# A gated state-space and product-key mixture on one core: one-hot products as 64-row products on the two row halves

## Chip, core and metric

The kernel runs on one core of one Trainium2 chip. The metric is device time in microseconds (us) of one execution. Before the change it is 1450.14 us, the median of 3 runs (1449.04 to 1450.3).

## The reference, cut to what matters

Two branches of the same 2048 tokens of 576 channels are mixed by a gate. Branch A is a diagonal state-space convolution of length 2048, branch B picks for each token and each of 32 heads 2 of 4096 experts by product keys:

```
s1, s2 = q1 @ k1.T, q2 @ k2.T             # 64 scores each, top 2 of each
top_e, g = best 2 of the 4 sums, softmax   # e = 64 * i1 + i2
act = gelu(x @ u[top_e])
out_B = sum over 32 heads and 2 picks of g * act * v[top_e]
out = sigmoid(x . gate_w) * out_A + (1 - gate) * out_B
```

The kernel doesn't gather experts. It computes x @ u.T for all 4096 experts, applies gelu, multiplies by a matrix of weights G[token, expert] that is zero but for the picked experts, and multiplies the result by all of v.

## The kernel before, in words

The program is written in Python that keeps its own clock: helpers add to it what each product should cost (`mm`, L207), tasks are generators that wait on that clock (`ready`, `need`), and so the order of each engine's instructions is fixed when the program is built. A changed cost or a changed duration in this model moves instructions.

Matmuls on TensorE carry short names in the profile: `a` is x @ u.T, `s` the scores of the product keys, `kP`, `kb`, `k`, `u`, `pr`, `pi`, `pv`, `y` belong to branch A's convolution, `tr` turns the picked indices and weights, `S` makes the matrix G, and `o` is the last product, with v. Until about 995 us `s`, `a` and branch A's stages share TensorE. After that it runs `o`, token block by token block (16 blocks t of 128 tokens, 32 groups b of 128 experts, three products for high and low parts, two halves of 288 columns), and between the `o` of one block it makes the `S` of a later one.

For a block t, `prep(t)` (L1498) loads gl, the 128 x 4096 values of x @ u.T, applies gelu, and goes through four quarters q of 32 tokens. For each quarter `onehot(t, q)` (L1485) lets VectorE write three tables. Partitions hold the picks: those of 16 tokens of the block's first half on partitions 0 to 63 (32 heads x 2 picks), those of 16 tokens of its second half on partitions 64 to 127. A is the one-hot of 128 row indices, Be the one-hot of the column index, and Bg is Be times the high and times the low part of the pick's weight. Be and Bg are 64 columns wide: `iota_b` is shifted by 32 in the lower partitions, so that a pick of partitions 0 to 63 can only hit columns 0 to 31 and one of partitions 64 to 127 only columns 32 to 63. One product with all 128 rows and 64 columns therefore makes G for two tokens. A quarter has 16 such pairs of tokens with two products each (high and low, accumulated), 32 in a block, in two PSUM banks (`pS`). VectorE then multiplies gl by them straight from PSUM, four instructions of 256 elements a quarter, and frees the banks. Two banks of tag `wb` are needed for a quarter, four are there. Tables of quarter q + 2 are written after quarter q's multiplications. At the end gl is split in f16 high and low parts, wh, the weights of `o`.

Of the kernel before, what the change touches and what calls it, by code (L numbers as in the profile page):

```python
# [13 lines left out]
F16 = mybir.dt.float16  # L14
# [4 lines left out]
OP = mybir.AluOpType  # L19
# [119 lines left out]
def body(ctx: ExitStack, tc: tile.TileContext, xT, au, par, logdt, dskip, gatew, wq, kT, uT, vv,  # L139
# [17 lines left out]
    def key(x):  # L157
        n = x.tensor.name
        return (n, x.offset) if n in columns else n

    def size(x):
        n = 1
        for d in x.shape[1:]:
            n *= d
        return n
# [30 lines left out]
    S = Engine(nc.scalar, rdy, clock, key, act_cost)  # L196
    V = Engine(nc.vector, rdy, clock, key, dve_cost)
    G = Engine(nc.gpsimd, rdy, clock, key, lambda op, o, a, k: 0.15 + 0.0021 * size(o))

    def dma(o, i, q=None):  # L200
        t = max(clock[0], rdy.get(key(i), 0.0), queue[0])
        queue[0] = t + 0.45
        wire[0] = max(wire[0], t) + (2 if o.dtype in (F16, BF16) else 4) * o.shape[0] * size(o) / 3.4e5
        rdy[key(o)] = max(rdy.get(key(o), 0.0), wire[0] + 2.2)
        (q or DQ).dma_start(o, i)

    def mm(o, l, r, start, stop, cost=None):  # L207
        m = l.shape[0] > 64, 128 if size(l) > 64 else size(l)
        if m != tiling[0]:
            tiling[0] = m  # L210
            clock[0] += 0.13 if m == (True, 128) else 0.1
        clock[0] += (size(r) * (4 if r.dtype == F32 else 1) / 2400 + 0.003) if cost is None else cost
        rdy[key(o)] = clock[0] + 0.4
        T.matmul(o, l, r, start=start, stop=stop)  # L214

    def spawn(gen, after=0.0):
        heapq.heappush(heap, (clock[0] + after, nseq[0], gen))
        nseq[0] += 1
# [49 lines left out]
    def take(tag, name):  # L268
        lst = slots[tag]
        assert lst, name  # L270
        lst.remove(min(lst))
# [18 lines left out]
    def bank(tag, name):  # L290
        take(tag, name)
        t = ps.tile([128, 512], F32, tag="ps", name=name, bufs=8)
        banks.add(t.tensor.name)
        return t
# [30 lines left out]
    cst = cp.tile([128, KT], F32, name="cst")  # L325
# [652 lines left out]
    ab = iota_a = iota_b = None  # L978
# [286 lines left out]
    def freq():  # L1265
        nonlocal ff, ab, iota_a, iota_b
        ff = FG.__enter__()
        wrems.append(ff.tile([128, 2, 512], F16, name="wrem3"))
        V.memset(wrems[3][64:128, 1, :], 0.0)
        ksb = KS.__enter__().tile([128, 4, NCK // 2, 32, 2 * NI], F16, name="ksb")  # L1270
        fk = FK.__enter__()
        tabs = [fk.tile([128, 16, 2, 128], F16, tag="tk", name=f"tk{w0}", bufs=2) for w0 in (0, 16)]
        for w0, tkt in zip((0, 16), tabs):
            dma(tkt, tk_d[:, w0:w0 + 16, :])
        for j in range(4):
            while wire[0] > clock[0] + 2:
                yield 0.3
            dma(ksb[:, j].rearrange("p c w i -> p c (w i)"),
                k_d[:, 32 * j:32 * j + 32].rearrange("c l z m n -> (l z m) c n"))
        spawn(v_norm(), 12)  # L1280
        spawn(gating(0), 20)
        yield from k_stage1(ksb, fk, tabs)
        FK.__exit__(None, None, None)
        KS.__exit__(None, None, None)
        v_pool(0, 3)
        spawn(v_work())
        fp = FP.__enter__()
        quota(sc=3, wb=5)
        yield 3
        spawn(prep(0))  # L1290
        yield from products(fp)
        FP.__exit__(None, None, None)
        quota(sc=4, wb=4)
        ab = ctx.enter_context(tc.tile_pool(name="ab", bufs=1, side="right"))
        iota_a = ab.tile([128, 128, 2], F16, name="iota_a")
        iota_b = ab.tile([128, 64, 2], F16, name="iota_b")
        V.tensor_copy(iota_a, cst[:, 384:512, None].to_broadcast([128, 128, 2]))
        V.tensor_copy(iota_b, cst[:, 512:576, None].to_broadcast([128, 64, 2]))
        iotas.append(1)
        v_pool(3, 5)  # L1300
        while not gated or not gates:
            yield 0.5
        FG.__exit__(None, None, None)
        WJ.__exit__(None, None, None)
        v_pool(5, 8)
        shut.append(1)
# [178 lines left out]
    def onehot(t, q):  # L1485
        def ib(r, m):
            v = idxT[:, t, r, 16 * q:16 * q + 16].rearrange("p (a k) -> p a k", k=2)
            return v[:, :, None, :].to_broadcast([128, 8, m, 2])
        A = ab.tile([128, 8, 128, 2], F16, tag="A1", name=f"A1{t}_{q}", bufs=2)
        V.tensor_tensor(out=A, in0=iota_a[:, None].to_broadcast([128, 8, 128, 2]), in1=ib(0, 128), op=OP.is_equal)  # L1490
        Be = ab.tile([128, 8, 64, 2], F16, tag="Be", name=f"Be{t}_{q}", bufs=1)
        V.tensor_tensor(out=Be, in0=iota_b[:, None].to_broadcast([128, 8, 64, 2]), in1=ib(1, 64), op=OP.is_equal)
        Bg = ab.tile([128, 2, 8, 64, 2], F16, tag="Bg", name=f"Bg{t}_{q}", bufs=2)
        for z in range(2):
            V.tensor_tensor(out=Bg[:, z], in0=Be, in1=ib(2 + z, 64), op=OP.mult)
        return A, Bg

    def prep(t):  # L1498
        while stored[t // 4] < 32 or groups:
            yield 1  # L1500
        yield from need("slot", 2)
        gl = [slot([16, 128], F32, f"gl{t}_{h}") for h in range(2)]
        for h in range(2):
            dma(gl[h], g_d[t][:, 16 * h:16 * h + 16])
        if t != ORDER[0]:
            while t not in placed:
                yield 0.3
            oh = {0: onehot(t, 0), 1: onehot(t, 1)}
        yield from ready(*gl)
        for h in range(2):  # L1510
            for b0 in (0, 8):
                g = gl[h][:, b0:b0 + 8]
                S.activation(g, g, AF.Gelu_apprx_tanh)
        if t == ORDER[0]:
            while t not in placed or not iotas:
                yield 0.3
            oh = {0: onehot(t, 0), 1: onehot(t, 1)}
        for q in range(4):
            A, Bg = oh.pop(q)
            yield from ready(A, Bg)  # L1520
            yield from need("wb", 2)
            pbs = []
            for hb in range(2):
                pS = bank("wb", f"S{t}_{q}_{hb}")
                for j in range(8):
                    a, k = 4 * hb + j // 2, j % 2
                    for z in range(2):
                        mm(pS[:, 64 * j:64 * j + 64], A[:, a, :, k], Bg[:, z, a, :, k], z == 0, z == 1)
                pbs.append(pS)
                del pS  # L1530
            yield from ready(*pbs)
            for hb, pS in enumerate(pbs):
                n0 = 16 * q + 8 * hb
                pv = pS.rearrange("p (k r b) -> p b r k", r=2, b=32)
                for h in range(2):
                    gv = gl[h].rearrange("p b (r n) -> p b r n", r=2)[:, :, :, n0:n0 + 8]
                    V.tensor_tensor(out=gv, in0=pv[:, 16 * h:16 * h + 16], in1=gv, op=OP.mult)
                free("wb", *gl)
            del pbs, pS, pv
            if q < 2:  # L1540
                oh[q + 2] = onehot(t, q + 2)
        if t != ORDER[-1]:
            spawn(prep(ORDER[ORDER.index(t) + 1]))
        h = []
        for z in range(2):
            yield from need("slot")
            h.append(slot([32, 128], F16, f"wh{t}_{z}"))
        fl = lambda x: x.rearrange("p b n -> p (b n)")
        for q in range(4):
            bs = slice(8 * q, 8 * q + 8)  # L1550
            src = gl[q // 2][:, 8 * (q % 2):8 * (q % 2) + 8]
            if t in ORDER[:2] and V.free > clock[0] + 6 and max(G.free, S.free) < clock[0] + 1:
                S.activation(fl(h[0][:, bs]), fl(src), AF.Copy, scale=s_wg)
                S.activation(fl(src), fl(src), AF.Copy, scale=s_wg)
                yield from ready(h[0], *gl)
                G.tensor_sub(fl(h[1][:, bs]), fl(src), fl(h[0][:, bs]))
            else:
                yield from split(fl(h[0][:, bs]), fl(h[1][:, bs]), fl(src), s_wg)
            yield 0.3
        free("slot", h[1])  # L1560
        free("slot", h[1])
        st[t] = h
# [147 lines left out]
    for w, n in ((0, 9), (1, 5)):  # L1710
        for xk in [x for k in range(4) for x in (k, 4 + k)[:2 - w]] + [8]:
            k = 4 if xk == 8 else xk % 4
# [12 lines left out]
    while groups or acts:  # L1725
# [5 lines left out]
        if groups and bank_free() and lag < (6.0 if not a_ok else 2.0 if not turn_s else 5.0 if kdone[0] < NCK else 8.0):  # L1731
            c, t = groups[0]
# [9 lines left out]
        if acts and bank_free():  # L1742
            c, tb, j = acts[0]
# [31 lines left out]
    for t in ORDER:  # L1775
        until(lambda: t in st)
        h = st.pop(t)
# [70 lines left out]
```

## Time and profile before

| | |
|---|---|
| median of 3 runs | 1450.14 us |
| lowest, highest | 1449.04, 1450.3 us |
| span of the profiled execution, first to last instruction | 1447.6 us |
| TensorE products / loads | 14105 / 14105 |
| S products | 2048 in 64 blocks, between 955 and 1391 us |
| o products | 3072 |

The profiled execution is one of its own; its time beside the span is not recorded, and its span is 2.5 us below the median of the runs. In the rows of the profile PE is TensorE's products, PEld its weight loads, DVE is VectorE, ACT ScalarE, POOL GpSimd. A group's row gives the tile written and those read, the shape, the count, then busy us, the mean ns of one, and the idle time of the engine just ahead of it with what ended it. In a product's shape `128*128` stands for the rows and columns of the weights. Ends of matmuls are modelled.

### The profile page before, as it was taken

The numbers are of one execution on the slowest core, as the hardware profiler recorded it, in microseconds if no ns is written. First come the engines' busy times: TensorE is split into PE (matmuls) and PEld (weight loads), VectorE is DVE, ScalarE is ACT, GpSimd is POOL, SyncE is SP. The second block draws the span as 40 slices with busy tenths as digits, with TensorE's granted clock in tenths as the row PEclk, the third lists the DMA queues.
The fourth block names the chain that finished last, engine by engine and source line by source line (L and its number), as shares of the span: only waits on it lengthen the run. The fifth ranks groups of instructions, "written<-read, shape, count | busy, mean of one in ns | idle before, by whom it ended". The sixth has DMA issues, their size and how long they took to land.

```text
span 1447.6 us, 36680 instructions
## 1 busy us (share of the span) xinstructions
PE 1426.9 (99%) x14105; PEld 852.3 (59%) x14105; DVE 1208.5 (83%) x4598; ACT 769.6 (53%) x1285; POOL 481.5 (33%) x491
## 2 busy tenths in 40 slices
PE   7999999999999999999999999999999999999998
PEld 3444445455455445445555444456887887888787
DVE  6899899889877997885899897589999988888850
ACT  6346876796684776844656655655434223323310
POOL 0325357547356436220547899600000000000000
PEclk9999999999999999999999999999999999999999
DMA  8235323342324333169675777776543333342400
GB/s 308 74 117 159 96 74 120 125 143 72 117 93 150 95 105 99 49 199 293 209 272 179 255 256 270 267 259 210 196 127 111 108 120 107 123 145 68 157 10 17
DMA packets 134351, 215.42 MB, mean 149 GB/s; under 512 B 10912, under 2 KB 79904, under 8 KB 127776
## 3 DMA queue, kind: packets, MB, share of 16 engines
q1 hardware_dynamic: 134080, 213.01, 45.5%
q8 instruction: 110, 1.80, 0.5%
q14 instruction: 65, 0.53, 0.1%
q10 hardware_dynamic: 96, 0.07, 0.0%
HBM read 141.74 MB, written 71.30 MB: 147 GB/s over the span
## 4 chain that ended last, share of the span: by engine, by line
PE 89%; DMA 2%; DVE 2%; issue 0%; ACT 0%; SPq 0%; ACTq 0%; DVEq 0%
PE o L214 26%; PE s L214 24%; PE a L214 23%; PE S L214 4%; PE kb L214 2%; PE pr L214 2%; PE wb L214 2%; PE y L214 1%; PE kP L214 1%; PE pv L214 1%; PE u L214 1%; PE k L214 1%; DMA z_d<-vo 1%; DMA ksb<-k_d 1%; DVE i L134 1%; DMA vn<-in_au_dram 0%
## 5 line engine op out<-in xcount | busy, mean ns | idle before, releaser
L214 PE MATMUL o<-vhl,wh 128*128 128x288 f16 x3072 | 387.0, 286 | 0.0
L214 PE MATMUL s<-whl,xb 128*128 128x512 f16 x1536 | 363.9, 379 | 0.0
L214 PE MATMUL a<-xb,uhl 128*128 128x512 f16 x1536 | 359.7, 379 | 0.2 <-DVE go L134 0.2
L214 PEld LDWEIGHTS <-wh 128*128 128x128 f16 x3072 | 296.0, 98 | 76.3 <-issue 3.7
L214 PEld LDWEIGHTS <-xb 128*128 128x128 f16 x1792 | 170.6, 98 | 210.1 <-issue 15.3
L214 PEld LDWEIGHTS <-uhl 128*128 128x128 f16 x1536 | 147.3, 98 | 176.2 <-issue 3.4
L134 DVE FIND_INDEX8 i<-m,s 128x8 uint32<-128x64 f32 x1024 | 206.5, 222 | 0.0
L134 ACT ACTIVATE wh<-gl,s_wg 128x1024 f16<-128x1024 f32 x64 | 68.9, 1137 | 202.3 <-DVE gl L134 202.3
L134 DVE MAX8 m<-s 128x8 f32<-128x64 f32 x1024 | 146.3, 215 | 29.3 <-PE s L214 28.4
L134 POOL TENSOR_TENSOR CS<-CS,ex 128x512 f32<-128x512 f32 x72 | 98.0, 1393 | 147.6 <-DVE ex L134 146.2
L134 ACT ACTIVATE go<-a,i_a 128x512 f32<-128x512 f32 x94 | 63.2, 685 | 96.4 <-PE a L214 68.6
L134 DVE TENSOR_TENSOR gl<-S,gl 128x256 f32<-128x256 f32 x256 | 90.5, 416 | 12.6 <-PE S L214 8.3
L134 POOL TENSOR_TENSOR e<-aN,rt 128x512 f32<-128x512 f32 x72 | 83.2, 1177 | 49.9 <-PE kb L214 43.7
L134 DVE SCALAR_TENSOR_TENSOR wh<-gl,s_wg,wh 128x1024 f16<-128x1024 f32 x63 | 78.6, 1280 | 10.7 <-ACT wh L134 10.7
L134 DVE TENSOR_TENSOR Bg<-Be,vals 128x1024 f16<-128x1024 f16 x128 | 84.6, 702 | 2.2
L134 ACT ACTIVATE gl<-gl 128x1024 f32<-128x1024 f32 x64 | 63.5, 1045 | 34.2 <-DMA gl<-g_d 31.1
L134 DVE TENSOR_TENSOR A<-iota_a,vals 128x2048 f16<-128x2048 f16 x64 | 77.9, 1216 | 0.0
L214 PE MATMUL s<-wrem,xb 128*128 128x512 f16 x256 | 76.2, 379 | 0.0
L214 PE MATMUL a<-xb,wrem 128*128 128x512 f16 x256 | 75.9, 379 | 0.0
L214 PEld LDWEIGHTS <-A 128*128 128x128 f16 x2048 | 70.5, 97 | 4.7
L134 DVE MATCH_VALUE_LOAD i<-m,s 128x8 f32 x1024 | 72.6, 71 | 0.1
L214 PE MATMUL S<-Bg,A 128*128 128x64 f16 x2048 | 72.3, 193 | 0.0
(205 smaller groups left out, 2068.5 us busy)
## 6 DMA issues: line engine op xcount, KB each, us to landing
g_d<-go SPq DMA_DIRECT2D x128, 256.0 KB, 2.5
gl<-g_d SPq DMA_DIRECT2D x32, 1024.0 KB, 5.4
wq<-in_wq_dram SPq DMA_DIRECT2D x16, 1152.0 KB, 6.0
su_d<-us SPq DMA_DIRECT2D x32, 288.0 KB, 2.6
sk_d<-k1o SPq DMA_DIRECT2D x32, 288.0 KB, 2.9
ui<-su_d SPq DMA_DIRECT2D x16, 576.0 KB, 4.0
ki<-sk_d SPq DMA_DIRECT2D x16, 576.0 KB, 5.3
vn<-in_vv_dram SPq DMA_DIRECT2D x32, 288.0 KB, 5.4
```

Of the source, the lines that this page charges most:

```text
L134: return f(*a, **k)
L214: T.matmul(o, l, r, start=start, stop=stop)
```

## The change

The two halves of the partitions are multiplied apart. A product uses 64 rows, of partitions 0 to 63 or 64 to 127, and 32 columns, and makes G for one token; there are 64 products a quarter instead of 32, those of the upper rows writing one bank and those of the lower rows the other, by turns. The second tables Be and Bg are 32 columns wide, since a half no longer needs the zero columns of the other, and `iota_b` is the same in all partitions. The order within a block is: token pair, high or low part, row half. The helper is given 0.014 us as the cost of one product. The multiplications of gl go over one bank for each row half, 16 x 16 elements, still four of 256.

```diff
-        iota_b = ab.tile([128, 64, 2], F16, name="iota_b")
+        iota_b = ab.tile([128, 32, 2], F16, name="iota_b")
...
-        V.tensor_copy(iota_b, cst[:, 512:576, None].to_broadcast([128, 64, 2]))
+        V.tensor_copy(iota_b, cst[:, 384:416, None].to_broadcast([128, 32, 2]))
...
-        Be = ab.tile([128, 8, 64, 2], F16, tag="Be", name=f"Be{t}_{q}", bufs=1)
-        V.tensor_tensor(out=Be, in0=iota_b[:, None].to_broadcast([128, 8, 64, 2]), in1=ib(1, 64), op=OP.is_equal)
-        Bg = ab.tile([128, 2, 8, 64, 2], F16, tag="Bg", name=f"Bg{t}_{q}", bufs=2)
+        Be = ab.tile([128, 8, 32, 2], F16, tag="Be", name=f"Be{t}_{q}", bufs=1)
+        V.tensor_tensor(out=Be, in0=iota_b[:, None].to_broadcast([128, 8, 32, 2]), in1=ib(1, 32), op=OP.is_equal)
+        Bg = ab.tile([128, 2, 8, 32, 2], F16, tag="Bg", name=f"Bg{t}_{q}", bufs=2)
         for z in range(2):
-            V.tensor_tensor(out=Bg[:, z], in0=Be, in1=ib(2 + z, 64), op=OP.mult)
+            V.tensor_tensor(out=Bg[:, z], in0=Be, in1=ib(2 + z, 32), op=OP.mult)
...
-            for hb in range(2):
-                pS = bank("wb", f"S{t}_{q}_{hb}")
-                for j in range(8):
-                    a, k = 4 * hb + j // 2, j % 2
-                    for z in range(2):
-                        mm(pS[:, 64 * j:64 * j + 64], A[:, a, :, k], Bg[:, z, a, :, k], z == 0, z == 1)
-                pbs.append(pS)
-                del pS
+            pbs = [bank("wb", f"S{t}_{q}_{r}") for r in range(2)]
+            for j in range(16):
+                for z in range(2):
+                    for r, pS in enumerate(pbs):
+                        rows = slice(64 * r, 64 * r + 64)
+                        mm(pS[:, 32 * j:32 * j + 32], A[rows, j // 2, :, j % 2], Bg[rows, z, j // 2, :, j % 2],
+                           z == 0, z == 1, 0.014)
             yield from ready(*pbs)
-            for hb, pS in enumerate(pbs):
-                n0 = 16 * q + 8 * hb
-                pv = pS.rearrange("p (k r b) -> p b r k", r=2, b=32)
+            n0 = 16 * q
+            for r, pS in enumerate(pbs):
+                pv = pS.rearrange("p (k b) -> p b k", b=32)
                 for h in range(2):
-                    gv = gl[h].rearrange("p b (r n) -> p b r n", r=2)[:, :, :, n0:n0 + 8]
+                    gv = gl[h].rearrange("p b (r n) -> p b r n", r=2)[:, :, r, n0:n0 + 16]
                     V.tensor_tensor(out=gv, in0=pv[:, 16 * h:16 * h + 16], in1=gv, op=OP.mult)
                 free("wb", *gl)
```

## Prediction

> **What bounds the kernel now.** I read the page first: busy shares and the chain that ended last.
>
> ```profile
> PE 1426.9 (99%) x14105; PEld 852.3 (59%) x14105; DVE 1208.5 (83%) x4598; ACT 769.6 (53%) x1285; POOL 481.5 (33%) x491
> PE 89%; DMA 2%; DVE 2%; issue 0%; ACT 0%; SPq 0%; ACTq 0%; DVEq 0%
> L214 PE MATMUL o<-vhl,wh 128*128 128x288 f16 x3072 | 387.0, 286 | 0.0
> L214 PE MATMUL S<-Bg,A 128*128 128x64 f16 x2048 | 72.3, 193 | 0.0
> core 0: 1447.6 us, clock 1.000
> ```
>
> The last number of the two group rows is the idle time of TensorE ahead of them: 0.0. The one-hot products S and the products o around them never wait for VectorE, though VectorE is nearly as full. The table by stage, for the stretch in which tokens are done one after another:
>
> ```profile
> 1015.00:1100.00 85.00, 85.00 (x1062) 68.82 (x1061) 82.51 (x140) 30.99 (x33) 0.00 (x0) 1.00 0.41 131
> 1200.00:1300.00 100.00, 100.00 (x1197) 81.22 (x1188) 88.68 (x146) 29.61 (x30) 0.00 (x0) 1.00 0.39 128
> ```
>
> The columns are length, PE, PEld, DVE, ACT, POOL, clock. A busy PE is not PE at its peak, so I price it by the chain, where each piece has its length from end to end. First the last token's blocks and the run behind them:
>
> ```profile
> 1380.76 0.97 PE S L214 x32
> 1381.73 3.68 PE o L214 x30
> 1385.41 0.97 PE S L214 x32
> 1391.02 52.93 PE o L214 x432
> ```
>
> An o product of 288 columns costs 52.93/432 = 0.1225 us, an S product of 64 columns 0.97/32 = 0.0303 us, and going from one to the other costs nothing. So TensorE sets the end alone, with no slack: what a quarter's block of S products gains or loses is gained or lost by the kernel, 64 times (16 tokens, 4 quarters). What VectorE saves is worth nothing unless TensorE waits for it.
>
> **The change part by part.** *The products.* A block was 32 products on the whole array; now it is 64 of 32 columns, in 32 pairs, one of each pair on rows 0 to 63 and one on rows 64 to 127. On TensorE, where the first of these blocks stands between o products, there was (A the weights; S names quarter and bank):
>
> ```order
> L214 LDWEIGHTS wh_1_13027
> L214 MATMUL o_1_13396<-vhl_12499,wh_1_13027 128x288
> L214 LDWEIGHTS A_0_13414
> L214 MATMUL S_0_0_13633<-Bg_0_13418,A_0_13414 128x64
> L214 LDWEIGHTS A_0_13414
> ```
>
> and at the same place now, with bank 0 and bank 1 by turns, each product behind a load of its own:
>
> ```order
> L214 LDWEIGHTS wh_1_13130
> L214 MATMUL o_1_13668<-vhl_9653,wh_1_13130 128x288
> L214 LDWEIGHTS A_0_13642
> L214 MATMUL S_0_0_13769<-Bg_0_13646,A_0_13642 128x32
> L214 LDWEIGHTS A_0_13642
> L214 MATMUL S_0_1_13770<-Bg_0_13646,A_0_13642 128x32
> ```
>
> Loads and products both double, 4096 of each. The number of blocks stays 64, each between o or a products, never beside another tiled block.
>
> The kernel has one stage with this very shape, the first stage of u: 64 rows, 128 columns of weights, two banks by turns. The chain there, with one more tiled block (kb, four column tiles) behind it:
>
> ```profile
> 373.93 1.51 PE s L214 x7
> 375.44 0.84 PE u L214 x12
> 376.28 1.83 PE s L214 x8
> 378.12 1.92 PE kb L214 x128
> ```
>
> Two things come out of it. The halves do run beside each other: 12 products of 288 columns cost 0.84 us, where 12 alone would cost 12 x 0.1225 = 1.47 and six 0.735. And entering and leaving a tiled block costs: u has 0.84 - 0.735 = 0.105 too much, and the s behind it 1.83 against 8 x 1.51/7 = 1.726, again 0.105. Together **0.21 us a block**, paid 64 times, that was not paid before.
>
> *The pitch of a pair.* The moving side needs less: by s (1.51/7 = 0.2157 for 512 columns) and o (0.1225 for 288) a column costs 0.416 ns, so 32 columns come to 0.1225 - 256 x 0.000416 = 16 ns. But no full-array product in the trace comes that close to the last one. The narrowest have one column:
>
> ```profile
> 123.32 0.19 PE L214 MATMUL wn<-sc,onesb 128*128 128x1 bf16 x2
> 123.38 0.38 PE L214 MATMUL a<-xb,uhl 128*128 128x512 f16 x1
> L214 PE MATMUL wn<-sc,onesb x32: 163/165/169, 30.7 to 783.8; 128*128 128x1 bf16 x32
> L214 PEld LDWEIGHTS <-tu x192: 92/94/97, 97.7 to 633.8; 64*128 64x128 f16 x192
> L214 PEld LDWEIGHTS <-A x2048: 96/97/99, 955.2 to 1390.8; 128*128 128x128 f16 x187
> ```
>
> Two of them end 0.19 us after the first began and one lasts 0.165, so the second starts 25 ns later; by the start of the a behind them it is (123.38 - 123.32)/2 = 30 ns. Something other than the moving columns, the load of 128 weight columns or the start itself, sets 25 to 30 ns on one set of rows. A load of 64 rows (tu, 94 ns) is hardly shorter than one of 128 (A, 97 ns), so halving the rows should not lower it. Both ends of the range for a pair: 16 ns (columns alone) and 56 ns (the loads of both halves in turn); I take **28 ns**, between the 25 and 30 of the one-column products and under the 30.3 that S has now, whose own columns (64 x 0.416 + 3) take almost that. kb speaks for the halves' loads not standing in each other's way: 128 loads and 128 products in 1.92 us, 15 ns for both.
>
> The block is then 32 x 0.028 + 0.21 = 1.106 us instead of 0.97: **+0.136 us, 64 times +8.7 us.** With 25 ns it would be +2.6, with 30.3 +13.4.
>
> The Trainium skill, "TensorEngine Tiling", section Instruction Overhead, speaks against the change: every matmul carries about 60 cycles whatever its width, so a dimension that is already small should not be cut further. Taken for each product by itself a block would be 64 x 0.0303 + 0.21 = 2.15 us, and the kernel 75 us slower; kb's 15 ns a product does not agree, as far as tiles beside each other go.
>
> *The tables.* VectorE's rows between 955 and 1392 us:
>
> ```profile
> L134 DVE TENSOR_TENSOR gl<-S,gl 128x256 f32<-128x256 f32 x256 | 90.5, 416 | 12.6 <-PE S L214 8.3 <-issue 3.8
> L134 DVE TENSOR_TENSOR Bg<-Be,vals 128x1024 f16<-128x1024 f16 x124 | 82.0, 703 | 2.2
> L134 DVE TENSOR_TENSOR A<-iota_a,vals 128x2048 f16<-128x2048 f16 x62 | 75.4, 1216 | 0.0
> L134 DVE TENSOR_TENSOR Be<-iota_b,vals 128x1024 f16<-128x1024 f16 x62 | 42.5, 685 | 0.0
> ```
>
> A and Be are the same operation at 2048 and 1024 elements: (1216 - 685)/1024 = 0.52 ns an element. Be and both Bg lose 512 each, so a quarter loses 3 x 0.266 = 0.80 us (1.04 if they simply halve), 51 to 67 us of VectorE in all. On the path: nothing, since TensorE waits for none of it. The multiplications of gl keep 256 elements, four a quarter; I keep their price.
>
> *The order.* Shorter tables let the scheduler put the products earlier. On VectorE, between quarter 0's and quarter 1's multiplications of a token, there stood
>
> ```order
> L134 TENSOR_TENSOR gl_1_17229<-S_0_1_17367,gl_1_17229 128x32x8
> L134 TENSOR_TENSOR A_2_17394<-iota_a,vals 128x2048
> L134 TENSOR_TENSOR Be_2_17396<-iota_b,vals 128x1024
> L134 TENSOR_TENSOR Bg_2_17398<-Be_2_17396,vals 128x1024 x2
> L134 TENSOR_TENSOR gl_0_17228<-S_1_0_17408,gl_0_17228 128x32x8
> ```
>
> and now
>
> ```order
> L134 TENSOR_TENSOR gl_1_18638<-S_0_1_18746,gl_1_18638 128x16x16
> L134 TENSOR_TENSOR A_2_18822<-iota_a,vals 128x2048
> L134 TENSOR_TENSOR Be_2_18824<-iota_b,vals 128x512
> L134 TENSOR_TENSOR Bg_2_18826<-Be_2_18824,vals 128x512 x2
> L134 TENSOR_TENSOR gl_0_18637<-S_1_0_18829,gl_0_18637 128x16x16
> ```
>
> The sequence is the same, the tables half as wide. On TensorE 6, 30 and 18 o products now stand between the four blocks of most tokens, where 12, 30 and 30 (or 6, 36 and 30) stood. Whether quarter 3 still finds its tables:
>
> ```profile
> 1378.17 1.13 PE L214 MATMUL S<-Bg,A 128*128 128x64 f16 x32
> 1387.09 1.29 DVE L134 TENSOR_TENSOR Bg<-Be,vals 128x1024 f16<-128x1024 f16 x2
> 1389.89 1.13 PE L214 MATMUL S<-Bg,A 128*128 128x64 f16 x32
> ```
>
> They are done at 1388.38, 1.51 us ahead. Now quarter 3 comes 54 x 0.1225 + 3 x 1.106 = 9.93 us after quarter 0 instead of 11.72, 1.79 earlier, and its tables 2 x 0.80 earlier less 0.136 for the longer first block: 1.51 - 1.79 + 1.60 - 0.14 = 1.2 us ahead. No wait arises. No DMA is moved in these stages.
>
> Sum: the span of 1447.6 becomes 1456.3. It lies 2.5 us below the median of the runs, 1450.14; with that around it I forecast **1458.8 us**.
>
> **The rivals.**
>
> *Faster: the columns set the pitch.* If what holds the one-column products does not hold a half, because each half's next load is done while the other half runs, a pair costs 16 ns, and a block 0.51 + 0.21 = 0.72: 64 x -0.25 = -16 us, 1434. It decides as soon as a pair falls below (0.97 - 0.21)/32 = 23.8 ns. For it: kb's 15 ns a product. Against: each of kb's four tiles has 1.92/32 = 60 ns between its own products, so it shows no tile running that fast. Chance 0.10.
>
> *No change: a pair at about 25 ns.* The lower reading of the one-column products; block 1.01 us, +2.6 us, 1452.7. A measurement of this kernel tells about 0.2% (2.9 us) from no change; that is a pair between 22.3 and 25.2 ns. The Trainium skill, "TensorE: Matmul & The Clock Gate", section "Wait — 56ns, not 53.3ns?", puts the floor from start to start at about 25 ns however narrow the product; by it this case would be the likeliest. Chance 0.14.
>
> *Much slower: the halves take turns.* That is the change not doing what it says. In u the two halves' loads had 122 ns to hide in; here they have 28. If they come one after another, a pair costs 56 ns, a block 2.00 us, and the kernel 64 x 1.03 = 66 us more: 1516. Chance 0.09.
>
> *VectorE becomes the wait.* gl now reads a bank at a stride of 32 with rows of 16. If each took 0.3 us longer, eight of them before quarter 3's tables eat the 1.2 us and 1.2 more, 16 times: +19 us, 1478. TensorE would then stand idle ahead of S. Nothing in the rows asks for it. Chance 0.04.
>
> **How the numbers follow.** The forecast's mechanism (a pair between 25.2 and some 38 ns) has 0.63. The range takes in it, the case of no change from 1447 (a pair at 22.3 ns, -3 us) and the wait for VectorE; its upper end of 1480 is a pair at 38 ns with the halves partly in each other's way. Left out are the fast pair and the halves in turn, 0.19. Faster 0.10, same 0.14, slower 0.63 + 0.09 + 0.04 = 0.76.
>
> **What would show it.** In the chain of the changed kernel S pieces with 64 products of about 0.9 to 1.0 us, the rest of the 1.106 in the o piece behind them; the idle of S and o still 0.0; VectorE's Be and Bg near 420 to 440 ns. S pieces of 0.5 to 0.6 us make the first rival right, near 1.9 the third; idle ahead of S, released by DVE, the fourth. The forecast is wrong in its core if entering and leaving costs less than 0.21 us or a pair under 24 ns.

## The result, and the profile after

The changed kernel takes 1452.92 us (median of 20 runs, 1451.21 to 1456.98), the kernel before beside it 1450.32 us (20 runs). The ratio is 1.0016, interval 1.0009 to 1.0024: 1.3 to 3.5 us slower. It was forecast 8.7 us slower; what came is the rival of a pair at about 25 ns, +2.6 us.

The page of the changed kernel, busy shares, chain and the largest group:

```profile
PE 1429.2 (98%) x16151; PEld 840.8 (58%) x16153; DVE 1158.4 (80%) x4601; ACT 766.3 (53%) x1282; POOL 479.5 (33%) x490
PE 88%; DMA 3%; DVE 2%; issue 0%; ACT 0%; SPq 0%; POOL 0%; DVEq 0%; ACTq 0%; POOLq 0%
L214 PE MATMUL o<-vhl,wh 128*128 128x288 f16 x3072 | 387.6, 286 | 0.0
```

The S products among the groups of TensorE behind 930 us:

```profile
L214 PE MATMUL S<-Bg,A 64*128 64x32 f16 x4096 | 61.9, 173 | 0.0
```

And their loads, among the groups of loads by shape:

```profile
L214 PEld LDWEIGHTS <-A 64*128 64x128 f16 x4096 | 55.6, 93 | 16.7 <-issue 13.1 <-DVE Bg L134 2.3 <-DVE vhl L134 0.8
```

TensorE still waits for nothing ahead of S and o (0.0), and VectorE has become emptier by 50 us. The chain through the last token's blocks is where the time is to be read:

```profile
1380.44 0.90 PE S L214 x64
1381.34 0.84 PE o L214 x6
1382.18 0.90 PE S L214 x64
1383.08 3.78 PE o L214 x30
1386.87 0.90 PE S L214 x64
```

Six o products alone cost 0.735 us, here 0.84; thirty 3.675, here 3.78. So leaving the tiled mode costs 0.105 us, as forecast. An S piece is 0.90 us; less 0.105 for entering, 0.795 are left for 32 pairs, **24.8 ns a pair** where the forecast had 28. In the single records of the trace the two products of a pair start 3 to 4 ns apart, and the next pair starts 25 ns after the last. A block costs 0.90 + 0.105 = 1.005 us against 0.97 before: +0.035, 64 times **+2.2 us**, which lies within the measured 1.3 to 3.5.

### The profile page after: what moved, and what is told of

The parts are those of the page before. It is cut to its first block, busy times and chain, and to the rows that moved or that the text cites. A ratio compares the mean times of both kernels' runs of the same rounds, so it can differ in the third digit from the quotient of the medians.

```text
span 1451.3 us, 40793 instructions
## 1 busy us (share of the span) xinstructions
PE 1429.2 (98%) x16151; PEld 840.8 (58%) x16153; DVE 1158.4 (80%) x4601; ACT 766.3 (53%) x1282; POOL 479.5 (33%) x490
## 4 chain that ended last, share of the span: by engine, by line
PE 88%; DMA 3%; DVE 2%; issue 0%; ACT 0%; SPq 0%; POOL 0%; DVEq 0%; ACTq 0%; POOLq 0%
PE o L214 26%; PE a L214 23%; PE s L214 23%; PE S L214 4%; PE kb L214 2%; PE pr L214 2%; PE wb L214 2%; PE pv L214 1%; PE y L214 1%; PE kP L214 1%; PE u L214 1%; PE k L214 1%; DMA wq<-in_wq_dram 1%; DMA ksb<-k_d 1%; DVE i L134 1%; DMA ui<-su_d 1%
## 5 line engine op out<-in xcount | busy, mean ns | idle before, releaser
L134 DVE SCALAR_TENSOR_TENSOR ya<-o,om,ya 128x288 f32<-128x288 f32 x32 | 15.2, 512 | 77.4 <-PE o L214 77.4
L214 PEld LDWEIGHTS <-A 64*128 64x128 f16 x4096 | 55.6, 93 | 16.7 <-issue 13.1
L134 ACT ACTIVATE CS<-CS 128x1024 f32<-128x1024 f32 x57 | 59.2, 1044 | 7.2 <-DVE CS L134 7.2
```

What stands on the lines that cost most here:

```text
L134: return f(*a, **k)
```

## The experiments

Theory A is the forecast's, with the pitch corrected: 25 ns a pair of products, 0.21 us for entering and leaving, TensorE alone sets the end. Against it stand B (the later time comes from the new order or from waits) and C (VectorE's relief hides part of the price). Within A two causes of the 25 ns compete: L, the load of the weights, and F, a limit on the starts of products.

**Products on all rows, 32 columns.**

```diff
-                    for r, pS in enumerate(pbs):
-                        rows = slice(64 * r, 64 * r + 64)
-                        mm(pS[:, 32 * j:32 * j + 32], A[rows, j // 2, :, j % 2], Bg[rows, z, j // 2, :, j % 2],
-                           z == 0, z == 1, 0.014)
+                    mm(pbs[j // 8][:, 32 * (j % 8):32 * (j % 8) + 32], A[:, j // 2, :, j % 2], Bg[:, z, j // 2, :, j % 2],
+                       z == 0, z == 1, 0.025)
...
```

Lines behind these, left out here, let VectorE read each product's columns for both tokens.

> Tables half as wide, but products on all 128 rows with 32 columns: 32 a quarter, no tiled mode. It leaves out the separation of the two tokens of a pair: their weights are added and used for both. Theory A: no entering and leaving; if a product on the full array also starts 25 ns after the last, a block is 0.80 us and the kernel 64 x -0.17 = 10.7 us faster than before, ratio 0.9926; if 28 ns (the reading of the one-column products), 0.90 us and 4.7 us faster, ratio 0.9968. Theory B: ratio near 1.0, since neither columns nor the mode would matter.

Measured: 1438.23 us against 1450.68, ratio 0.9914, 0.9899 to 0.9929. Its chain:

```profile
1308.25 0.79 PE S L214 x32
1309.05 1.48 PE o L214 x12
1310.52 0.79 PE S L214 x32
```

0.79/32 = 24.7 ns a product, and the 12 o products behind it cost what 12 cost (1.47): nothing is paid for entering or leaving. The forecast of 10.7 us lies in the interval, that of 4.7 us for 28 ns does not. So a single product on the whole array and a pair on the two halves have the same pitch, 25 ns, and what separates this kernel from the changed one is the 0.21 us of each block.

**The halves in turn.**

```diff
-            for j in range(16):
-                for z in range(2):
-                    for r, pS in enumerate(pbs):
-                        rows = slice(64 * r, 64 * r + 64)
+            for r, pS in enumerate(pbs):
+                rows = slice(64 * r, 64 * r + 64)
+                for j in range(16):
+                    for z in range(2):
```

> The changed kernel with the loops turned: all 32 products of the upper row half, then all 32 of the lower. If 25 ns is a limit of each row half (theory A as I hold it), a block has 64 steps of 25 ns, 1.60 + 0.21 = 1.81 us, and the kernel is 64 x 0.80 = 51 us slower than the changed one, about 1504 us. If the limit were one of TensorE's issue as a whole, at 12.5 ns a product, the order of the halves would not matter: about 1453 us.

Measured: 1498.09 us, one run.

```profile
1304.03 1.62 PE S L214 x64
1305.65 2.31 PE o L214 x18
```

(1.62 - 0.105)/64 = 23.7 ns a product on the average of a block. In the single records the products of one half start 25 ns apart; the average is lower because the first products of the lower half start beside the last ones of the upper, which is also why the time stays under the expected 1504 us. The limit is one of each row half; with the halves by turns both run at it, 12.4 ns a product over all. The rival in which the halves take turns by themselves is out.

**Columns: 16, and 64.**

```diff
-                        mm(pS[:, 32 * j:32 * j + 32], A[rows, j // 2, :, j % 2], Bg[rows, z, j // 2, :, j % 2],
+                        mm(pS[:, 16 * j:16 * j + 16], A[rows, j // 2, :, j % 2], Bg[rows, z, j // 2, 0:16, j % 2],
...
```

> The changed kernel with products of 16 columns instead of 32. It leaves out the upper 16 columns of each weight table; the lower ones are used twice. If the moving columns set the pitch of a pair, it falls (16 columns x 0.416 = 7 ns fewer, 18 ns); if a limit per product or per load of 128 weight columns sets it, it stays at 25 ns, S pieces of 0.90 us.

```diff
-                        mm(pS[:, 32 * j:32 * j + 32], A[rows, j // 2, :, j % 2], Bg[rows, z, j // 2, :, j % 2],
+                        mm(pS[:, 64 * (j // 2):64 * (j // 2) + 64], A[rows, j // 2, :, j % 2], Bg[rows, z, j // 2].rearrange("p b k -> p (b k)"),
```

> The changed kernel with products of 64 columns: both tokens of a neighbouring pair of columns at once, so that each token's sums are mixed with its neighbour's. The columns then need 64 x 0.416 + 2.7 = 29.3 ns. Under a limit of 25 ns per product the pitch of a pair becomes 29 to 30 ns, S pieces of about 1.04 us; if both limits add up, 25 + 13 = 38 ns and about 1.3 us.

Measured: 1452.34 us with 16 columns and 1462.09 with 64, one run each, the kernel before beside them 1449.27. An S piece of each:

```profile
1353.61 0.89 PE S L214 x64
```

```profile
1362.21 1.04 PE S L214 x64
```

Half the columns change nothing (24.5 ns), twice the columns give (1.04 - 0.105)/32 = 29.2 ns, the columns' own 29.3. The limits don't add up; the larger one holds. By an estimate from these numbers the moving columns matter only above some 54 columns (25 = 2.7 + 54 x 0.416); no run has a width between 32 and 64.

**One more load a product.**

```diff
                         rows = slice(64 * r, 64 * r + 64)
+                        T.ldweights(A[rows, j // 2, :, 1 - j % 2], tile_position=(64 * r, 0))
```

> The changed kernel with one more load of the same size ahead of each product (of other columns of A, then overwritten by the product's own load, so the result is the same). If the load of 128 weight columns sets the 25 ns (theory L), two loads double the pitch of a pair to about 50 ns: S pieces of about 1.7 us and a kernel 51 us slower. If a limit on the starts of products sets it and the load is hidden beneath (theory F), the pitch stays near 25 ns, at most 30. In between it would say that a load takes less than 25 ns but not nothing.

Measured: 1656.07 us, one run; far more than either theory had. F is out, a load is not hidden. But L's figure, some 50 ns a pair, is nearly met only in the first part of a block. The table by stage, over one block that began at 1385.01:

```profile
1385.00:1386.00 1.00, 1.00 (x34) 1.00 (x67) 1.00 (x3) 0.00 (x0) 0.00 (x0) 1.00 0.00 0
1386.00:1388.20 2.20, 2.20 (x38) 2.15 (x67) 0.58 (x1) 0.00 (x0) 0.00 (x0) 1.00 0.04 7
1100.00:1300.00 200.00, 200.00 (x2236) 158.22 (x3441) 107.05 (x199) 44.86 (x46) 0.00 (x0) 0.86 0.29 90
```

A block in the chain:

```profile
1343.11 3.08 PE S L214 x64
```

Some 34 products in the first microsecond are near 59 ns a pair. For the rest of the block, at the same granted clock, the single records show that the two halves no longer start together: one product starts every 64 ns. Over the whole stage the clock granted is 0.86 besides, and an o product lasts 310 ns on the mean of the kernel instead of 286. Why the halves fall out of step stays open: no run here tells it.

**96 columns of weights.**

```diff
-                        mm(pS[:, 32 * j:32 * j + 32], A[rows, j // 2, :, j % 2], Bg[rows, z, j // 2, :, j % 2],
+                        mm(pS[0:96, 32 * j:32 * j + 32], A[rows, j // 2, 0:96, j % 2], Bg[rows, z, j // 2, :, j % 2],
...
```

> The changed kernel with the first 96 of the 128 weight columns: the rows 96 to 127 of G are left out. In the trace of before a load of 96 columns (of Zp, 123 ns) lasts 26 ns longer than one of 128 (97 ns). Theory L (the load sets the 25 ns): the pitch of a pair grows by about that, to some 50 ns, and the kernel is some 50 us slower. Theory F (a limit on the starts of products, loads hidden): 25 ns as it is, time as the changed kernel.

Measured: 1497.23 us, one run; clock 1.000. The group of its loads:

```profile
L214 PEld LDWEIGHTS <-A 64*96 64x96 f16 x4096 | 100.3, 122 | 16.7 <-issue 14.9 <-DVE vhl L134 0.8 <-DVE ya L134 0.5
```

An S piece of its chain:

```profile
1361.07 1.59 PE S L214 x64
```

Fewer weight columns make the load longer, 122 ns instead of 93, and the pitch of a pair (1.59 - 0.105)/32 = 46 ns instead of 25, with the same moving columns and as many products. A limit on the starts of products could not do that. Nor do the halves take turns here, which would be 23 ns a product, near the time of the halves in turn: in the single records the two products of a pair start 3 to 4 ns apart, as in the changed kernel, and the next pair 46 to 47 ns after the last. L holds: **the load of the weights sets the pitch.** The Trainium skill, "TensorE: Matmul & The Clock Gate", section "Weight-path perf modes — Fast Weight Load (FWL) and DoubleRow", says that the fast load is used when there are 128 weights and the type is not FP32; the runs agree, 93 and 122 ns.

**The tables as wide as before.**

```diff
-        Be = ab.tile([128, 8, 32, 2], F16, tag="Be", name=f"Be{t}_{q}", bufs=1)
+        Be = ab.tile([128, 8, 64, 2], F16, tag="Be", name=f"Be{t}_{q}", bufs=1)
...
-                        mm(pS[:, 32 * j:32 * j + 32], A[rows, j // 2, :, j % 2], Bg[rows, z, j // 2, :, j % 2],
+                        mm(pS[:, 32 * j:32 * j + 32], A[rows, j // 2, :, j % 2], Bg[rows, z, j // 2, 0:32, j % 2],
...
```

> The changed kernel's products with the second tables as wide as before (64 columns, of which the products use the first 32): VectorE has its 51 to 67 us more to do again. Theory A (TensorE alone sets the end): as the changed kernel within 1 us, ratio to before 1.0010 to 1.0025, and no idle time ahead of S. Theory C (the shorter tables gave something back that hides part of the price of the tiled products): slower than the changed kernel by several us, with idle time of TensorE ahead of S that VectorE ends.

Measured: 1452.56 us, ratio to before 1.0014, 1.0004 to 1.0025: the changed kernel's time. VectorE's Bg is back at 688 ns (its group between 955 and 1395 us), and TensorE waits 0.4 us for it once (the waits of TensorE behind 930 us, in total, times, longest):

```profile
L134 DVE TENSOR_TENSOR Bg<-Be,vals 128x1024 f16<-128x1024 f16 x124 | 80.2, 688 | 2.1
```

```profile
PE S L214 <- DVE Bg L134: 0.4, 1, 0.4
```

The changed kernel itself can wait as long: in the trace of its repeat below, TensorE stands idle ahead of S twice, 0.7 us in all. Some 50 us of VectorE's work (busy 1208.1 us here, 1158.4 in the changed kernel) go or stay without a difference in the time that these runs could tell. C is out.

**Two quarters a visit.**

```diff
-        for q in range(4):
-            A, Bg = oh.pop(q)
-            yield from ready(A, Bg)
-            yield from need("wb", 2)
-            pbs = []
-            pbs = [bank("wb", f"S{t}_{q}_{r}") for r in range(2)]
+        for q0 in (0, 2):
+            yield from ready(*oh[q0], *oh[q0 + 1])
+            yield from need("wb", 4)
+            four = []
+            for q in (q0, q0 + 1):
+                A, Bg = oh.pop(q)
+                pbs = [bank("wb", f"S{t}_{q}_{r}") for r in range(2)]
...
```

> The products of quarters 0 and 1 stand back to back, and those of 2 and 3: 32 visits to the tiled mode instead of 64, all else as in the changed kernel. Theory A (25 ns a pair plus 0.21 us for entering and leaving, nothing else): a visit costs 64 x 0.025 + 0.21 = 1.81 us, 32 of them 57.9 us, against 64.3 us in the changed kernel (64 x 1.005) and 62.1 us before (64 x 0.97): 6.4 us faster than the changed kernel, 4.2 us faster than the kernel before, ratio to it about 0.997. Theory B (the pitch is not the point, the later time comes from the new order or from waits elsewhere): about as the changed kernel, ratio about 1.0016.

Measured: 1448.99 us, ratio 0.9991, 0.9980 to 1.0002: less than expected. A visit costs what A says (the chain), but two of them had to wait (the waits of TensorE between 930 and 1445 us, in total, times, longest):

```profile
1356.55 1.70 PE S L214 x128
1358.24 8.93 PE o L214 x72
```

```profile
PE S L214 <- DVE Bg L134: 1.3, 2, 0.9
PE o L214 <- issue: 0.4, 1, 0.4
```

1.70 us, and 8.93 - 72 x 0.1225 = 0.11 behind it: 1.81 as worked out. The two lengths also part the pitch from the price of entering: 1.70 us for 64 pairs less 0.90 for 32 is 25 ns a pair, which leaves 0.10 us for entering. The waits, 0.9 us for tables of the second token and 0.4 for those of the third, are new. They are about half of what is missing to the expected 4.2 us. Two further versions put the visits later in the model's clock:

```diff
-            yield from ready(*oh[q0], *oh[q0 + 1])
+            yield from ready(*oh[q0], *oh[q0 + 1], late=1.2)
```

> The kernel with two quarters a visit, each visit put 1.2 us later in the model's clock, so that the tables are there when TensorE comes. Theory A: no idle time of TensorE ahead of S, 32 visits x 1.81 us = 57.9 us against 62.1 before: 4.2 us faster than before, ratio 0.997, and 6.4 us faster than the changed kernel of the same call. If the first version's missing 2 to 3 us had another cause than waits for tables, the ratio stays near 0.999.

Measured: 1448.52 us, ratio 0.9999, 0.9988 to 1.0010. A wait of 1.0 us for Bg was there again, now at the third token; the expectation missed. That wait is only a quarter of the 4 us that are missing here; what took the rest is not shown.

```diff
-            yield from ready(*oh[q0], *oh[q0 + 1])
+            yield from ready(*oh[q0], *oh[q0 + 1], late=4.0 if t in ORDER[1:3] else 0.4)
```

> Two quarters a visit, with the visits of the second and third token put 4 us later in the model's clock (the others 0.4 us), where both versions so far had TensorE wait some 1 to 1.5 us for the tables. Theory A: no wait left inside the visits, 32 x 1.81 = 57.9 us against 62.1 before, 4.2 us faster than before, ratio 0.997. If a wait turns up at another place, it gives back what it lasts.

Measured: **1446.39 us, ratio 0.9978, 0.9969 to 0.9986**, against 1449.75: faster than before by 2.0 to 4.5 us, and so faster than both kernels. All that TensorE waits for between 925 us and the end is

```profile
PE o L214 <- issue: 0.6, 1, 0.6
```

**The changed kernel once more.**

> The changed kernel once more, beside the other version on one chip. Theory A, with the pitch of 25 ns that its trace shows: 64 x (0.90 + 0.105 - 0.97) = 2.2 us slower than before, ratio 1.0015. Nothing in it should differ from the first runs.

Measured beside the version put 1.2 us later: 1452.81 us, ratio 1.0024, 1.0013 to 1.0035. The expected 1.0015 lies in it. B is out. With half the visits and no waits inside them the kernel takes 1446.39 us against 1452.81 and 1452.92, 6.4 us less, which is what half the visits cost; the two versions with waits took 1448.99 and 1448.52, some 4 us less. And the products on all rows, with no tiled blocks, take some 14 us less than the changed kernel, of which 64 x 0.21 = 13.4 us are the price of the blocks' entering and leaving.

## Why the prediction was wrong, point by point

- *What bounds the kernel*: right. Idle ahead of S and o is 0.0 again, and wide tables cost nothing.
- *Entering and leaving, 0.21 us a block, from u's chain*: right, 0.105 twice, and absent where the products use all rows.
- *The halves run beside each other*: right, shown by the version in turn.
- **The pitch of a pair, 28 ns: the step that failed.** It is 24.8 ns. The forecast took it from one-column products, which are of another shape: 25 by one reading, 30 by the other. The single records of the trace before don't settle it either: the second of two such products starts 28 ns after the first in 12 of 16 cases, and the product behind it mostly 25 to 26 ns after the second. 3.2 ns on 32 pairs are 0.10 us a block, 6.5 of the 8.7 us. The cause I named for it, "the load of 128 weight columns or the start itself", is the load. The term was the difference of two nearly equal sums (0.97 and 1.106), so that 9% of one of them was three quarters of the result. The measured time lies in the range, but not near the forecast.
- *No change, a pair at about 25 ns*: this rival came. The Trainium skill, "TensorE: Matmul & The Clock Gate", section "Wait — 56ns, not 53.3ns?", has this number. The runs agree for 16 and 32 columns on 128 weight columns (24.5 and 24.8 ns), but only among products on the same row half: those of the two halves start 3 to 4 ns apart. With 96 weight columns the pitch is 46 ns, so here it is the load that sets it.
- *Columns alone set the pitch (faster)*: no; 16 columns run as 32.
- *Each product pays by itself* (the Trainium skill, "TensorEngine Tiling", section Instruction Overhead): the runs don't agree where tiles run beside each other; two halves pay 24.8 ns for both.
- *Tables*: Be and Bg at 419 and 422 ns against 419 and 437 forecast. Off the path, as said.
- *Quarter 3's tables 1.2 us ahead*: right for one token (1.3 us in the single records), far off for the next, and so by turns through the steady stretch; without effect. The last token's rows:

```profile
1381.43 0.42 DVE L134 TENSOR_TENSOR gl<-S,gl 128x256 f32<-128x256 f32 x1 [1.04 <-ACT gl L134]
1382.98 1.09 DVE L134 TENSOR_TENSOR gl<-S,gl 128x256 f32<-128x256 f32 x3 [1.12 <-ACT gl L134]
1389.16 0.76 DVE L134 TENSOR_TENSOR Bg<-Be,vals 128x512 f16<-128x512 f16 x2
1390.01 0.97 PE L214 MATMUL S<-Bg,A 64*128 64x32 f16 x64
```

They are ready at 1389.92, 0.09 us ahead. VectorE waited for the gelu of gl on ScalarE, which I had not looked at. Before the change the last piece of it ran ahead of quarter 0's products, which began at 1378.17:

```profile
1372.67 2.00 ACT L134 ACTIVATE gl<-gl 128x1024 f32<-128x1024 f32 x2 [3.59 <-DMA gl<-g_d]
```

Now it runs beside them (quarter 0's block begins at 1380.44), behind a wait of ScalarE for ya:

```profile
1378.38 0.78 ACT L134 ACTIVATE ya<-ya,gA 128x576 f32<-128x576 f32 x1 [9.17 <-DVE ya L134]
1379.06 3.88 ACT L134 ACTIVATE gl<-gl 128x1024 f32<-128x1024 f32 x4
```

A little more would have had TensorE wait for VectorE, as in the fourth rival, though by another cause.

## What to carry to other kernels

Splitting a product on the row halves pays only if its moving columns were what took the time: here a full product of 64 columns took 30.3 ns, and the load beneath it 25, so that 18% could be won a block and 0.21 us for the change of mode ate more than that. Gather as many tiled products as banks allow into one visit, since the price is one of the visit and not of the product. When a forecast is the small difference of two sums, take the pitch from a row of the same shape, or, where there is none, forecast the band that the readings of the nearest one leave.

## What the runs showed of the hardware that had not been expected

The two row halves load and multiply fully side by side: 64 loads and 64 products in 0.795 us, 12.4 ns for one of each. A load of 96 weight columns is slower than one of 128 (122 against 93 ns; a pair 46 against 25). A second load ahead of each product costs much more than its share: 3.08 us a block instead of 0.90, with the two halves out of step from the middle of a block on, and a clock of 0.86 over the stage.
